# Routed expert tiles: weights split by two engines instead of three, one chunk in eight as float32

## The chip, the cores and the metric

The kernel runs on one core of a Trainium2 chip. The core has a matrix engine (TensorE, PE in the profile), three engines for elementwise work (VectorE or DVE, ScalarE or ACT, GpSimd or POOL) and SyncE (SP), whose queue issues DMAs. The metric is the time on the device in microseconds; lower is better.

## The reference

Three stages in float32: softmax attention with rotary embedding, a dense layer with softplus, and a layer in which each token whose skip score is positive goes to one of eight experts. Only the last is touched by the change:

```python
e_idx = np.argmax(xc @ w_gate, axis=1)
for e in range(E):                       # E = 8, D = 512, F = 1024
    mask = e_idx == e
    h = np.maximum(xc[mask] @ w1[e], 0.0)
    y[mask] = gate_w[mask, None] * (h @ w2[e])
out[do_compute] = xc + y
```

## The kernel before

TensorE multiplies in float32r, which keeps fewer bits than float32. So each operand is split in a high part (its float32r rounding) and a low part (the difference), and each product is three matmuls: high by high, low by high, high by low.

Attention and the dense layer take about the first 470 us. Then the tokens are sorted into tiles of 128, each of one expert (`Moe2.tiles`); nine tiles are computed. Tile 0 is begun early (`moe2.early`, lines 1156 to 1165 and 1191), tiles 1 to 8 follow in the loop of lines 960 to 979. For each tile:

- `next_w` and `load_w` load the expert's weights in eight chunks of 128 x 1024 numbers, 512 KB each, into the buffers `raw[0]` to `raw[7]`, one per chunk: 0 to 3 for the first product (L811), 4 to 7 for the second (L815). All go through SP's queue in this order: chunks 0 to 3 of the next tile, then chunks 4 to 7 of this one. A load is skipped when the expert is that of the tile before. A load waits until the buffer's last reader is done.
- `fetch` gathers the tokens' rows by an indirect DMA of GpSimd (L844), up to three tiles ahead; `gather` transposes them on TensorE (L855) and splits them (L859: high on ScalarE, low on VectorE).
- `split_w` splits each chunk into a tile `ws`. For tiles 1 to 8 the high part is a cast on ScalarE (L832), but for chunks 2, 4 and 6 on VectorE (L830). The low part is a subtraction (L836) on GpSimd for chunks 1, 3 and 5 and on VectorE for the others. The split tiles live in rings of buffers: six for chunks 0 to 3, six for 4 to 7.
- `hidden_mm` is the first product (L864): 24 matmuls of 512 columns, three for each of four chunks and two halves. `relu` (L882, ScalarE) and `turn` (transposes L893, split L895 and L896) follow.
- `result` is the second product (L910), 24 matmuls of 512 columns. `finish` makes the row numbers (L919) and the output rows (L921) on VectorE, and GpSimd scatters them by an indirect DMA (L922).

Each engine's order is not that of the text. The program is built with `schedule_with_timeline_sim=True`: a planner puts the instructions of each engine in an order by a simulated timeline, and what is under `issue_after(x)` comes after `x`. On the chip every engine then runs its list in order. In the loop, `hidden` of tile T is written before `result` of tile T - 1, and the planner mixes the two on TensorE.

Of the kernel before, what the change touches and what calls it, by code (L numbers as in the profile page):

```python
# [9 lines left out]
F32 = mybir.dt.float32  # L10
# [10 lines left out]
B, H, S, D = 2, 8, 576, 64  # L21
# [14 lines left out]
# the order in which the tiles of tokens are routed  # L36
ORDER2 = (4, 5, 6, 7, 8, 0, 1, 2, 3)
HI_DVE = (2, 4, 6)
LO_POOL = (1, 3, 5)
# [9 lines left out]
class Attention:  # L49
    """Softmax attention of head pairs; leaves x^T, split in two float32r parts, in xh and xl."""  # L50

    def __init__(self, nc, q, k, v, cst, xh, xl, pools):
        self.nc, self.q, self.k, self.v, self.cst, self.xh, self.xl = nc, q, k, v, cst, xh, xl
        self.nat, self.wq, self.wp, self.wk, self.ps_s, self.ps_t, self.ps_pv = pools
        self.pr = {}
        self.rem, self.rot = {}, {}
        self.un = {}
        self.pt = {}
        self.pv, self.sums = {}, {}
        self.qm = []  # L60
        for i in range(2):
            t = self.wq.tile([128, 2, 128], F32R, name=f"qm{i}", tag=f"qm{i}", bufs=1)
            nc.vector.memset(t.bitcast(F32), 0.0)
            nc.vector.tensor_copy(t, t.bitcast(F32))
            self.qm.append(t)
        # order of the units (query tiles of 128; "m" holds the last 64 queries of both heads)
        self.order = {0: [0, 1, 2, 3, "m"], 1: [2, 3, "m", 0, 1]}
        self.chunks = {0: [[0, 1], [2, 3, "m"]], 1: [[2, 3], ["m", 0, 1]]}
# [18 lines left out]
    # ---- loads  # L87
# [28 lines left out]
    # ---- rotary embedding  # L116
    def _rope(self, engs, out, x, tmp, cos, sin):
        """out = x * cos + swap(x) * sin, the last dimension being that of a head; the tables broadcast over heads."""
# [26 lines left out]
    # ---- transposed q, k in two parts  # L145
    def halves(self, hi, lo, src, q=False):
        """The two parts of src, which for q is scaled by 1 / sqrt(D)."""
# [30 lines left out]
    def stacks(self, b, hp):  # L178
        """Both heads' operands with K = 128: [high q; low q] against [high k; high k]."""
# [19 lines left out]
    # ---- one unit: scores, softmax  # L199
    def s_mm(self, b, hp, u, a):  # L200
# [15 lines left out]
        if (b, hp) == (0, 0) and u < 2:  # L216
            # before the stacks are there
# [41 lines left out]
    def where(self, b, u):  # L259
        """The chunk of a unit, the chunk's whole units, and where the unit's queries start in it."""  # L260
# [8 lines left out]
    def norm(self, b, hp, c):  # L269
        """1 / (sum + 1e-9) of a chunk, transposed from the rows of squares."""  # L270
# [23 lines left out]
    # ---- transposes of the probabilities, in parts, as emitters  # L294
    def t_steps(self, b, hp, u):
# [46 lines left out]
        def mk(g):  # L342
            def pe():
# [14 lines left out]
                else:  # L358
# [3 lines left out]
                    if str(g) in POOL_T[self.stage(4 * b + hp)][z]:  # L362
                        # the general purpose engine doesn't read the transposes where they are
# [15 lines left out]
    def place(self, c, i):  # L379
        """Where the chunk's two-part transposes keep block i."""  # L380
        return i if c else i - 3 * sum(3 * g < i for g in WHOLE)

    # ---- P V of one head and one chunk of queries
# [36 lines left out]
    # ---- the whole, software pipelined  # L420
    def warm(self, n, part):
        """Keeps the tensor engine's clock up while the first inputs arrive and are made ready."""
# [72 lines left out]
    def prepare(self, i, pairs):  # L495
        """What the next pair of heads needs, spread over the units of this one."""
# [24 lines left out]
class Moe1:  # L521
    """x @ w_in, softplus, @ w_out; the float64 weights are read as pairs of 32 bit words."""
# [7 lines left out]
    def weights(self, f, wp, st, bufs):  # L530
        """Loads the weights of 128 hidden units and leaves them in two float32r parts."""
# [3 lines left out]
        for i in range(2):  # L535
# [11 lines left out]
            # the float32 that keeps the first 24 bits: sign and first exponent bit, last 7 exponent bits, mantissa  # L547
# [8 lines left out]
    def hidden(self, ci, f, hp, tp, gq):  # L556
# [19 lines left out]
        # narrow chunks leave room for the logarithm beside its argument  # L576
# [9 lines left out]
        # log1p(y) = ln(u) + (y - (u - 1)) for u = y + 1 as rounded  # L586
# [29 lines left out]
class Moe2:  # L616
    """Top-1 routing of the tokens with a positive skip score; tiles of 128 tokens of one expert each."""
# [30 lines left out]
    def logits(self, t, xt, ps_a, tag="ra"):  # L648
        """Gate logits and skip score of one tile of tokens."""
# [8 lines left out]
    def route(self, t0, n, ps_a, more=None):  # L658
        """Expert, gate and rank within the expert for the tiles t0 .. t0 + n."""
# [11 lines left out]
        # the first expert among those with the largest logit, none for the tokens that skip  # L671
# [10 lines left out]
        # number of the row, zero for the tokens that skip  # L682
        nc.gpsimd.tensor_single_scalar(act, sk, 0.0, op=ALU.is_gt)
        nc.gpsimd.tensor_mul(self.tok[:, ts_, 0], c["row1"][:, ts_], act[:, :, 0])
        # ranks: earlier tokens of the tile, then of the earlier tiles
# [21 lines left out]
        # start of every tile less the full tiles of earlier tokens; token number at its place in a tile  # L707
# [14 lines left out]
        # the gate and the token's number go to the end of its row  # L722
# [13 lines left out]
    def first_tile(self, ps_a):  # L736
        """The first tile of the first expert takes tokens of the tiles routed so far; what it lacks stays empty."""
# [18 lines left out]
    def starts(self, ps):  # L756
        """Where the tokens of every expert start, and where the last ones end."""
# [12 lines left out]
    def slots(self, cum, ps_a, more):  # L770
        """The tokens of every tile and the experts of the tiles."""
        nc, c, ST, sb = self.nc, self.cst, self.ST, self.sp
        # the tile of every token: that which starts where the expert does, and the full tiles of earlier tokens on
# [6 lines left out]
        # token numbers of every tile and place; empty slots read some row and write none  # L780
# [9 lines left out]
        # experts of the tiles and their number  # L790
# [26 lines left out]
    def load_w(self, e, part, **kw):  # L817
        """Half of the weights of expert e; with a condition they may stay what they are."""
# [3 lines left out]
    def split_w(self, T, c, raw=None):  # L822
        nc = self.nc
        raw = self.raw[c] if raw is None else raw
        wp, n = self.ring[2 if c > 3 and (T, c) != (0, 4) else 0 if (c if T == 0 else 4 * T - 4 + c) % 6 < 2 else 1]
        w = wp.tile([128, 2, 2, 512], F32R, name=f"ws{T}{c}", tag="w", bufs=n).rearrange("p x a n -> p x (a n)")
        late = (T, c) in ((0, 5), (0, 6), (0, 7))
        with self.tc.issue_after(self.ex.ins) if late else nullcontext():
            if T and c in HI_DVE:
                hi = nc.vector.tensor_copy(w[:, 0], raw)  # L830
            else:
                hi = nc.scalar.copy(w[:, 0], raw)  # L832
        with self.tc.issue_after(self.late[1]) if (T, c) in ((0, 6), (0, 7)) else nullcontext():
            pool = c in LO_POOL and (T, c) != (self.NT - 1, 6) if T else c in LO0
            eng = nc.gpsimd if pool else nc.vector
# [3 lines left out]
    def fetch(self, T, xp):  # L839
        """The rows of the tokens of tile T."""  # L840
# [9 lines left out]
    def gather(self, T, xp, ps_x, tag="x"):  # L850
# [8 lines left out]
        self.split = nc.scalar.copy(xt[0], ps).ins, nc.vector.tensor_sub(xt[1], ps, xt[0].bitcast(F32)).ins  # L859
# [7 lines left out]
    def hidden_mm(self, T, st, ph):  # L867
        nc, xt = self.nc, st[1]
        for k in range(4):
            w = self.early[k] if T == 0 else self.split_w(T, k)  # L870
            for z, (x, y) in enumerate(((0, 0), (1, 0), (0, 1))):
# [55 lines left out]
    def next_w(self, T):  # L927
        """The expert of tile T, and whether it is another one than that of the tile before."""
# [5 lines left out]
    def tiles(self, Ts, xp, ps_x, ps_y, ps_h, st=None):  # L934
        """The tiles Ts; st is what hidden() left of the first one, if it has been there."""
# [24 lines left out]
        for T in Ts:  # L960
            cur = nxt
            st = self.hidden(T, st, xp, [ps_h.tile([128, 512], F32, name=f"mh{T}{c}", tag="mh") for c in range(2)])
            with ExitStack() as order:
                if first:
                    # the weights of the next tile come before what isn't needed until later
                    for done in self.did[1, 1][0], self.did[1, 1][1], self.did[1, 0][1]:
# [16 lines left out]
def constants():  # L983
# [22 lines left out]
    # number of the token on partition p of tile t, and that of its row on the way (counted from 1)  # L1006
# [30 lines left out]
def out_rows(ap, t):  # L1037
    """The rows of the tokens on partitions 0 .. 127 of tile t."""
# [7 lines left out]
def attention_moe_moe_kernel(ctx: ExitStack, tc, q, k, v, w_in, w_out, w_skip, w_gate, w1, w2, tab, out):  # L1046
# [16 lines left out]
    with ExitStack() as s1:  # L1063
# [29 lines left out]
        with ExitStack() as s2:  # L1093
# [5 lines left out]
            # the first tokens take the hidden units in two halves, the others all of them in between  # L1099
# [22 lines left out]
            def second(group):  # L1122
                """@ w_out for some steps of one phase, token tile by token tile when there are several."""
# [111 lines left out]
```

## Time and profile before

| | us |
|---|---|
| median of 3 runs | 632.38 |
| lowest, highest | 628.38, 632.98 |
| span of the profiled execution | 637.8 |
| end of the last engine's work in it | 632.8 |

The profile is of one execution. Its span is 5.4 us above the runs' median, and its last 5 us hold no work of an engine, only the branches for tiles that are not needed. Times in the views count from the span's start. In a timeline row several instructions of one kind are merged: start, time from the first to the end of the last, and their count.

### The profile page before, as it was taken

Reading aid. Unit: us, or ns where it says so; the run is one execution under the profiler, and the core shown is the slowest. Engines: PE = TensorE matmul, PEld = TensorE weight load, DVE = VectorE, ACT = ScalarE, POOL = GpSimd, SP = SyncE. Lnnn points to the kernel's source line nnn. Section 1 sums busy time; section 2 is a strip of 40 time slices with the busy share of each in tenths; the row PEclk is TensorE's granted clock in tenths of the full one; section 3 lists DMA queues with packets and bytes.
Section 4 is the critical chain, followed back from the end, with each engine's and each line's share of the span. In section 5 each row is a group of like instructions: output and inputs, shape, how many; then the busy total and the mean of one; then the engine's idle time right before and its main releaser. Section 6 shows DMA issues by size and latency. Waiting matters only on the chain. (4 is left out here: it accounts for less than half of the span.)

```text
span 637.8 us, 9087 instructions
## 1 busy us (share of the span) xinstructions
PE 562.5 (88%) x2906; PEld 444.7 (70%) x2906; DVE 520.2 (82%) x857; ACT 346.2 (54%) x795; POOL 349.7 (55%) x317
## 2 busy tenths in 40 slices
PE   5898989999999989788987799999997697997785
PEld 2576767777777766667875698898875575666663
DVE  7389887988888999998699674536867879999894
ACT  1376657777777554455455565565544273543430
POOL 5778695878443656563445742212616366574452
PEclk9699769999999989797999799999999799988788
DMA  7666260432130232433033400040246123873000
GB/s 169 160 173 162 93 167 23 121 79 63 39 71 1 67 99 69 129 122 109 2 99 103 128 34 2 6 160 6 82 168 218 49 66 125 319 249 136 2 19 30
DMA packets 40457, 62.49 MB, mean 98 GB/s; under 512 B 9313, under 2 KB 23905, under 8 KB 40401
## 3 DMA queue, kind: packets, MB, share of 16 engines
q1 hardware_dynamic: 36624, 54.88, 29.0%
q0 software_dynamic: 1440, 4.20, 1.8%
q10 hardware_dynamic: 2336, 2.74, 1.4%
q8 instruction: 26, 0.43, 0.3%
q14 instruction: 31, 0.25, 0.1%
HBM read 67.30 MB, written 7.15 MB: 117 GB/s over the span
## 5 line engine op out<-in xcount | busy, mean ns | idle before, releaser
L566 PE MATMUL h<-xh,w 128*128 128x320 f32 (+2 forms) x448 | 109.9, 327 | 5.1 <-POOL w L553 2.3
L596 POOL TENSOR_TENSOR r<-r,y 128x320 f32<-128x320 f32 (+2 forms) x54 | 56.3, 1045 | 94.4 <-DVE y L593 68.3
L610 PE MATMUL acc<-w,gh 128*128 128x512 f32 x288 | 90.3, 420 | 11.8 <-ACT gh L600 9.2
L836 POOL TENSOR_TENSOR ws<-raw,ws 128x1024 fp32r<-128x1024 f32 x25 | 65.1, 2617 | 43.3 <-ACT ws L832 22.3
L566 PEld LDWEIGHTS h<-xh,w 128*128 128x128 f32 x448 | 79.7, 198 | 12.0 <-POOL w L553 3.1
L836 DVE TENSOR_TENSOR ws<-raw,ws 128x1024 fp32r<-128x1024 f32 x42 | 76.0, 1831 | 1.0 <-ACT ws L832 0.3
L910 PE MATMUL y<-ws,hT 128*128 128x512 f32 x216 | 62.7, 431 | 14.9 <-DVE ws L836 8.9
L610 PEld LDWEIGHTS acc<-w,gh 128*128 128x128 f32 x288 | 55.0, 199 | 26.3 <-ACT gh L600 13.2
L566 PE MATMUL h<-xl,w 128*128 128x320 f32 (+2 forms) x224 | 70.1, 324 | 0.0
L553 POOL TENSOR_TENSOR w<-wt,w 128x512 fp32r<-128x512 f32 x32 | 50.1, 1568 | 32.1 <-ACT w L552 29.2
L910 PEld LDWEIGHTS y<-ws,hT 128*128 128x128 f32 x216 | 41.8, 204 | 29.2 <-DVE ws L836 12.7
L400 PE MATMUL pv<-pt,vv 128*128 128x320 f32 (+3 forms) x272 | 59.1, 338 | 2.8 <-DVE x L412 2.4
L864 PE MATMUL mh<-ws,xgT 128*128 128x512 f32 x192 | 52.5, 417 | 8.6 <-DVE ws L836 6.5
L610 PE MATMUL acc<-w,gl 128*128 128x512 f32 x144 | 51.5, 404 | 9.1 <-DVE gl L601 9.1
L239 DVE TENSOR_REDUCE m<-s 128x1 f32<-128x576 f32 x64 | 48.0, 751 | 13.1 <-PE s L231 9.5
L598 DVE TENSOR_TENSOR r<-r,u 128x320 f32<-128x320 f32 (+2 forms) x56 | 40.5, 730 | 20.3 <-POOL r L596 19.6
L252 ACT ACTIVATE P<-s,m 128x576 f32<-128x576 f32 x64 | 48.0, 750 | 9.6 <-DVE m L239 9.0
L400 PEld LDWEIGHTS pv<-pt,vv 128*128 128x128 f32 (+1 forms) x272 | 42.6, 198 | 11.6 <-issue 4.7
L864 PEld LDWEIGHTS mh<-ws,xgT 128*128 128x128 f32 x192 | 36.5, 197 | 19.5 <-DVE ws L836 9.0
L322 PE MATMUL t<-ct,P 128*128 128x128 f32 x288 | 48.6, 298 | 1.2 <-DVE pt L317 0.7
L600 ACT CAST gh<-r 128x320 fp32r<-128x320 f32 (+2 forms) x56 | 25.9, 467 | 43.7 <-DVE r L598 43.7
L832 ACT CAST ws<-raw 128x1024 fp32r<-128x1024 f32 x43 | 43.9, 1054 | 4.2 <-DMA raw<-in_moe_w_dram 2.1
(266 smaller groups left out, 1240.1 us busy)
## 6 DMA issues: line engine op xcount, KB each, us to landing
raw<-in_moe_w_dram SPq DMA_DIRECT2D x68, 512.0 KB
raw<-in_moe_w_in_dram SPq DMA_DIRECT2D x16, 512.0 KB
raw<-in_moe_w_out_dram SPq DMA_DIRECT2D x16, 512.0 KB
ks<-kT SPq DMA_DIRECT2D x32, 144.0 KB
qs<-qT SPq DMA_DIRECT2D x32, 128.0 KB
wr<-in_moe_w_dram SPq DMA_DIRECT2D x5, 512.0 KB
x2d<-x SPq DMA_DIRECT2D x9, 256.0 KB
xn<-in_q_dram SPq DMA_DIRECT2D x8, 256.0 KB
```

Source lines behind the costliest of these rows:

```text
L239: nc.vector.tensor_reduce(st["m"][:, a : a + 1], st["ps"][a][:, :, 0:288], axis=AX.XY, op=ALU.max, negate=True)
L252: nc.scalar.activation(P[:, 576 * a : 576 * a + 576].rearrange("p (c n) -> p c n", c=2), ps[:, :, 0:288], AF.Exp, bias=m[:, a : a + 1], ac ...
L322: nc.tensor.transpose(ps[:, 128 * i : 128 * i + 128], src, ident)
L400: nc.tensor.matmul(ps[:, 0:n], lhsT=vv[r, i, :], rhs=pt[r, x, self.place(c, i), 0:n], **se)
L553: nc.gpsimd.tensor_sub(w[:, i, 1, :], t, h.bitcast(F32))
L566: nc.tensor.matmul(ps[c][:, 0:m], lhsT=w[:, 0, x, 128 * k : 128 * k + 128], rhs=src[:, k, c0 + m * c : c0 + m * c + m], start=z == 0, stop ...
L596: (nc.vector if ci == 3 and f in R_DVE else nc.gpsimd).tensor_sub(r[:, c], r[:, c], y[:, c])
L610: nc.tensor.matmul(acc[t], lhsT=g[x][:, 128 * j : 128 * j + 128], rhs=w[:, 1, y, :], start=f == f0 and z == 0, stop=f == f1 and z == 2,)
L832: hi = nc.scalar.copy(w[:, 0], raw)
L836: self.did[T, c] = hi.ins, eng.tensor_sub(w[:, 1], raw, w[:, 0].bitcast(F32)).ins
L864: mm()
L910: nc.tensor.matmul(py, lhsT=ht[:, x, o : o + 128], rhs=w[:, y, 512 * j : 512 * j + 512], start=c == 0 and j == 0 and z == 0, stop=c == 3 a ...
```

## The change

For tiles 1 to 8: chunk 0 (`NATIVE`) is no longer split. `gather` keeps the first 128 columns of the transposed rows as float32 (`xr`), and `hidden_mm` multiplies them with `raw[0]` as it was loaded, in two float32 matmuls instead of six float32r ones. For the seven other chunks the high part is always made by ScalarE and the low part always by VectorE. GpSimd makes low parts for tile 0's chunks only. The ring of six buffers for the first product is counted over three chunks a tile. One of three conditions on the order of tile 0's end goes away. The rest of the diff removes comments.

```diff
-HI_DVE = (2, 4, 6)
-LO_POOL = (1, 3, 5)
+NATIVE = (0,)
...
     def split_w(self, T, c, raw=None):
         nc = self.nc
         raw = self.raw[c] if raw is None else raw
-        wp, n = self.ring[2 if c > 3 and (T, c) != (0, 4) else 0 if (c if T == 0 else 4 * T - 4 + c) % 6 < 2 else 1]
+        if T and c in NATIVE:
+            return raw
+        n1 = [x for x in range(4) if x not in NATIVE]
+        at = c if T == 0 or c > 3 else len(n1) * (T - 1) + n1.index(c)
+        wp, n = self.ring[2 if c > 3 and (T, c) != (0, 4) else 0 if at % 6 < 2 else 1]
...
-            if T and c in HI_DVE:
-                hi = nc.vector.tensor_copy(w[:, 0], raw)
-            else:
-                hi = nc.scalar.copy(w[:, 0], raw)
+            hi = nc.scalar.copy(w[:, 0], raw)
...
-            pool = c in LO_POOL and (T, c) != (self.NT - 1, 6) if T else c in LO0
-            eng = nc.gpsimd if pool else nc.vector
+            eng = nc.gpsimd if T == 0 and c in LO0 else nc.vector
...
-        self.split = nc.scalar.copy(xt[0], ps).ins, nc.vector.tensor_sub(xt[1], ps, xt[0].bitcast(F32)).ins
+        o = 0
+        if T and NATIVE:
+            xr = xp.tile([128, 128], F32, name=f"xgT{T}r", tag="gr", bufs=2)
+            nc.scalar.copy(xr, ps[:, 0:128])
+            xt.append(xr)
+            o = 128
+        self.split = (
+            nc.scalar.copy(xt[0][:, o:], ps[:, o:]).ins,
+            nc.vector.tensor_sub(xt[1][:, o:], ps[:, o:], xt[0][:, o:].bitcast(F32)).ins,
+        )
...
             w = self.early[k] if T == 0 else self.split_w(T, k)
+            if T and k in NATIVE:
+                for c in range(2):
+                    yield partial(
+                        nc.tensor.matmul, ph[c], lhsT=xt[2], rhs=w[:, 512 * c : 512 * c + 512],
+                        start=k == 0, stop=k == 3,
+                    )
+                continue
...
-                    for done in self.did[1, 1][0], self.did[1, 1][1], self.did[1, 0][1]:
+                    for done in self.did[1, 1]:
```

## Rows read from the trace of the kernel before

**Rows 1.** The page's part 1: each engine's busy us, share, instructions.

```profile
PE 562.5 (88%) x2906; PEld 444.7 (70%) x2906; DVE 520.2 (82%) x857; ACT 346.2 (54%) x795; POOL 349.7 (55%) x317
```

**Rows 2.** Windows: stretch, busy us by engine, TensorE clock, DMA share, GB/s.

```profile
596.00:614.00 18.00, 15.16 (x56) 11.88 (x56) 15.99 (x13) 6.55 (x10) 8.61 (x5) 0.81 0.04 16
...
sum 139.00, PE 114.66 PEld 87.18 DVE 127.21 ACT 57.31 POOL 75.90; mean PE 14.33 PEld 10.90 DVE 15.90 ACT 7.16 POOL 9.49
```

**Rows 3.** Groups by line and shape, 493 to 632 us: count | busy us, mean ns | idle before.

```profile
L836 DVE TENSOR_TENSOR ws<-raw,ws 128x1024 fp32r<-128x1024 f32 x39 | 72.5, 1878 | 1.0 <-ACT ws L832 0.3
...
L832 ACT CAST ws<-raw 128x1024 fp32r<-128x1024 f32 x38 | 38.9, 1055 | 2.1 <-DMA raw<-in_moe_w_dram 2.1
...
L830 DVE CAST ws<-raw 128x1024 fp32r<-128x1024 f32 x24 | 29.9, 1244 | 0.0
...
L919 DVE TENSOR_TENSOR si<-xg,e 128x1 int32<-128x1 f32 x7 | 7.9, 1131 | 1.9 <-DMA xg<-x2d,gi 1.9
...
L859 DVE TENSOR_TENSOR xgT<-xgt,xgT 128x512 fp32r<-128x512 f32 x8 | 5.4, 680 | 0.0
```

**Rows 4.** Single durations in ns, min/median/max, of tile `ws`.

```profile
L864 PE MATMUL mh<-ws,xgT x192: 387/394/793, 493.5 to 613.7; 128*128 128x512 f32 x192
...
L836 DVE TENSOR_TENSOR ws<-raw,ws x42: 1208/1226/6194, 486.5 to 627.7; 128x1024 fp32r<-128x1024 f32 x42
...
L830 DVE CAST ws<-raw x24: 675/682/3405, 495.7 to 625.9; 128x1024 fp32r<-128x1024 f32 x24
```

**Rows 5.** Timeline, 591 to 598 us: start, us, engine, line, count [idle before].

```profile
591.27 5.39 POOL L836 TENSOR_TENSOR ws<-raw,ws 128x1024 fp32r<-128x1024 f32 x2
...
592.16 2.28 DVE L830 CAST ws<-raw 128x1024 fp32r<-128x1024 f32 x1
594.47 3.27 DVE L836 TENSOR_TENSOR ws<-raw,ws 128x1024 fp32r<-128x1024 f32 x1
...
597.80 2.92 PE L910 MATMUL y<-ws,hT 128*128 128x512 f32 x6 [2.10 <-DVE ws L836]
```

**Rows 6.** Groups by line, 493 to 632 us, TensorE's two products and their idle time.

```profile
L910 PE MATMUL y<-ws,hT 128*128 128x512 f32 x195 | 57.0, 434 | 14.5 <-DVE ws L836 8.9 <-DVE ws L830 3.3 <-POOL ws L836 2.0
L864 PE MATMUL mh<-ws,xgT 128*128 128x512 f32 x192 | 52.5, 417 | 8.6 <-DVE ws L836 6.5 <-DVE xgT L859 1.1 <-POOL ws L836 1.0
```

**Rows 7.** Timeline: relu pairs of tiles 2 and 8, the last scatter.

```profile
514.00 1.10 ACT L882 ACTIVATE hs<-mh 128x512 f32<-128x512 f32 x2
...
613.92 1.08 ACT L882 ACTIVATE hs<-mh 128x512 f32<-128x512 f32 x2 [7.08 <-PE mh L864]
...
631.80 0.98 POOL L922 DMA_INDIRECT out_dram<-yo,si  x1 [4.41 <-DVE yo L921]
```

**Rows 8.** Timeline, 486 to 489 us: a gather of GpSimd beside VectorE's low parts.

```profile
486.46 3.49 DVE L836 TENSOR_TENSOR ws<-raw,ws 128x1024 fp32r<-128x1024 f32 x3
...
486.50 2.05 POOL L844 DMA_INDIRECT xg<-x2d,gi  x1 [0.30 <-issue]
```

**Rows 9.** Timeline and line 397: matmuls of float32r, of float32, and transposes.

```profile
606.64 5.25 PE L864 MATMUL mh<-ws,xgT 128*128 128x512 f32 x22
...
35.11 1.51 PE L397 MATMUL pv<-pw,vr 128*64 128x256 f32 x6
...
L397 PE MATMUL pv<-pw,vr x48: 379/379/609, 35.1 to 206.1; 128*64 128x256 f32 x48
...
546.43 1.03 PE L893 MATMUL ht<-ct,hs 128*128 128x128 f32 x8
```

**Rows 10.** DMA, 470 to 638 us in 40 slices of 4.2 us; SP's longest waits there.

```profile
GB/s 174 84 125 72 311 400 102 0 4 0 0 10 241 173 205 0 33 375 351 294 272 300 245 346 54 0 153 346 2 5 0 2 0 66 0 2 6 62 34 16
...
SPq L811 <- DVE ws L836: 24.9, 10, 5.4
```

**Rows 11.** Timeline, 491 to 512 us: the start of tile 1.

```profile
491.96 2.59 DVE L919 TENSOR_TENSOR si<-xg,e 128x1 int32<-128x1 f32 x1 [1.87 <-DMA xg<-x2d,gi]
...
496.94 7.33 DVE L836 TENSOR_TENSOR ws<-raw,ws 128x1024 fp32r<-128x1024 f32 x2
```

## The prediction

> **What bounds the kernel now.** I read the page's busy shares first [rows 1]: TensorE 88%, VectorE 82%, GpSimd 55%, ScalarE 54%. A matmul's record overlaps the next one, so these shares don't name the bound, and the diff touches only tiles 1 to 8 of the routed layer. The windows view therefore comes next, over 493 to 632 us, where those tiles run [rows 2]. There VectorE is busy 127.2 of 139 us, TensorE 114.7, ScalarE 57.3. In 596 to 614 TensorE was granted 0.81 of its clock on average, and almost no weights arrive (16 GB/s).
>
> The groups by line in that stretch [rows 3] show that VectorE's 127.2 us are not work. The undisturbed price stands in the medians [rows 4]: a low part (L836) 1.226 us, a high part (L830) 0.682 us. Line 836 has 39 low parts, so 39 x 1.226 = 47.8 us, but it took 72.5: 24.7 us too many. Line 830 has 24 high parts, 16.4 us, but took 29.9: 13.5 too many. Line 919's seven indices have one column each and took 7.9 us; I count that as waiting too. Together 46 us of 127 are waiting inside instructions. The timeline says for what [rows 5]: GpSimd runs two low parts from 591.27 to 596.66. VectorE's cast that starts at 592.16 takes 2.28 us, and its low part at 594.47 takes 3.27 and ends 1.1 us after GpSimd's last. So VectorE is held for as long as GpSimd's low part runs. TensorE then has nothing to multiply until 597.80; 2.10 us of that wait are put down to the low part, and the six matmuls after it take 2.92 us, where six take 1.55 at the spacing of [rows 9]: after the wait the clock is at its lower level, 1.2 GHz. In total [rows 6] TensorE's matmuls of these tiles have 14.5 + 8.6 = 23.1 us of idle time in front of them, and 8.9 + 3.3 + 2.0 + 6.5 + 1.0 = 21.7 of it ends with a low or high part of the weights.
>
> **The change, part by part.** Marks for the sum are the relu pairs of tile 2 (514.00) and tile 8 (613.92), and GpSimd's last scatter, ending at 632.78 [rows 7]. Between the marks lie six tile steps, 99.9 / 6 = 16.65 us each.
>
> *GpSimd's low parts go to VectorE, VectorE's high parts to ScalarE.* VectorE's stretch becomes 127.2 - 29.9 (no high parts) - 24.7 (held low parts) - 7.9 (held indices) + 20.8 (56 low parts where 39 lay in the stretch, 17 x 1.226) - 1.2 (the low part of the rows, 0.68 us, shrinks to three quarters, seven times) = 84.3 us, about 10.5 a tile. That all of the excess goes is the assumption; the other end is that only line 830's goes with its instructions and the low parts stay held by something else: 84.3 + 32.6 = 117 us, 14.6 a tile. What GpSimd keeps is indirect DMAs, and beside one of 2.05 us three low parts took 3.49 us together, undisturbed [rows 8]; I take 10.5. ScalarE gets 16 more high parts of 1.055 us [rows 3] and eight copies of 128 columns, each below such a high part of 1024: at most 57.3 + 16.9 + 8.4 = 82.6 us, 10.3 a tile. It doesn't set the pace either. Its queue is in order, though: a high part that waits for its chunk holds up the relu behind it.
>
> *One chunk in eight as float32.* Six split matmuls go, two float32 ones come. 22 matmuls of 512 columns take 5.25 us from the first to the end of the last, whose record is 0.394 us [rows 4], so one follows the other every (5.25 - 0.394) / 21 = 0.231 us [rows 9], at the upper clock level. The nearest float32 price is line 397, 256 columns: 24 matmuls leave 48 records, six in a row take 1.51 us, (1.51 - 0.38) / 5 = 0.226 us a record, 0.45 a matmul. At 512 columns that is between 0.45 (if columns cost nothing) and 0.90 (in proportion); in proportion is nearer, since all else of TensorE's goes by columns. Two cost 1.81 us where six cost 1.39: 0.42 a tile more, with ends of -0.5 and +0.42. TensorE's floor per tile is then 42 x 0.231 + 1.81 + 12 transposes x 0.13 (eight in 1.03 [rows 9]) = 9.70 + 1.81 + 1.55 = 13.0 us.
>
> The Trainium skill, page "TensorE: Matmul & The Clock Gate", section "Back-to-back issue gap", gives a sustained spacing of about 131 ns for matmuls of 512 columns in a stream with their weight loads. By that the 42 split matmuls would take an estimated 5.5 us instead of 9.7, VectorE's 10.5 us a tile would set the pace, and six steps would be 6 x (14.2 - 10.5) = 22 us shorter than in the sum below; the rows here show 231 ns, and the measurement decides.
>
> *The wait that is added.* The float32 chunk is multiplied straight from the buffer that the load fills. So on TensorE tile T's first matmul waits for a landing where it waited for a split, with all else of TensorE behind it. And on SP the load of the next tile's chunk 0 waits for TensorE's matmuls of this tile, where it waited for VectorE's low part [rows 10]; behind it on SP stand chunks 1 to 3 of the next tile and chunks 4 to 7 of this one. The time to land is covered: the load is free 1.8 us into a tile of 13.0, and eight chunks of 0.524 MB, 4.19 MB, at the 245 to 375 GB/s of the seven full slices in a row (mean 312) take 13.4 us, ends 11 and 17 [rows 10]. That about equals TensorE's 13.0 us, so in three of the six steps (transfers lie in the slices from 520 to 588 us alone) I add 1.5 us; without that cover each would cost up to the whole 13.4.
>
> *The rings.* Three split chunks a tile in the six buffers for the first product instead of four reach two tiles ahead rather than one and a half; I count nothing for it, since VectorE and not a free buffer was late. The order of the first tile's end loses one condition (the low part of chunk 0, which is no longer made): nothing, as the remaining two come later.
>
> **The sum.** *Start:* two low parts at the head of tile 1 take VectorE 7.33 us where two undisturbed ones take 2.45, and an index before it took 2.59 us [rows 11]. Without the holds 4.9 + 2.6 = 7.5 us go, but loads still land until the slice that ends at 499 [rows 10]; I take 6 us at mark tile 2 (ends 2 and 9). *Six steps:* TensorE's 13.0, plus waits that remain, between 0 and today's 23.1 / 8 = 2.9 us a tile, of which I take 0.5, because 1.4 of the 23.1 us don't end with a part of the weights and ScalarE's queue is fuller, plus 0.75 for the loads (1.5 in half the steps): 14.2 us against 16.65, a gain of 14.7 (ends: 13.0, a gain of 22; 15.9, a gain of 4.5). *End:* from mark tile 8 to the last scatter 18.9 us; 48 matmuls are 11.1, relu 1.1 [rows 7], eight transposes 1.0 [rows 9], the scatter 1.0 [rows 7], the splits and output rows, three pieces like line 859's 0.68 us [rows 3], 2.0, together 16.2; I take a gain of 2.5 us (ends 0 and 3). Sum 6 + 14.7 + 2.5 = 23.2 us. It is made against the profiled execution, whose last work ends at 632.8 us and whose span is 637.8 [rows 7]; the runs' median is 632.4. I take the gain over unchanged: **609 us**.
>
> **The rivals.**
> - *TensorE sets the pace and never waits.* For it: once fed it runs 22 matmuls without a gap. Against: [rows 2] shows 15.2 us of overlapping records in a window of 18. 632.4 - 22 - 9 - 3 = 598 us.
> - *Chunk 0's load is late in the three tiles with new weights.* SP's queue puts both halves behind TensorE; for it, SP already waits 24.9 us for splits [rows 10]; against, the load takes 13.4 us and has a tile of 14.2. At 4 us for each of three tiles: 621 us.
> - *Load and product alternate, and it ends slower.* The place is the same: if a new tile's products start only when all its chunks have landed, and the planner puts TensorE's first matmul of the tile before behind the rest of that tile's work, three tiles pay the whole 13.4 us: 609 + 40 = 649 us. It decides from 8 us a tile on (three times 8 eat the gain). Against it: the second half of the weights is not needed until the next tile's first product is through.
> - *VectorE stays held* (117 us in the stretch, above): 14.6 a tile against 16.65, no head gain but that of the index: about 619 us.
> - *Gathers starve.* An indirect DMA of GpSimd took 2.05 us beside VectorE's low parts, the last scatter, with VectorE idle, 0.98 [rows 7, 8], and VectorE now runs more of them. Gathers are issued two tiles ahead, some 28 us, so a delay by a whole run of seven low parts, 8.6 us, stays hidden unless three add up; then one shows, 618 us. The Trainium skill, "SBUF — State Buffer", section "SBUF: two separate sides", has it that GpSimd can't write the descriptors of such a DMA while VectorE runs an operation that takes the port pair which both share.
> - *No change*: the order that the planner now writes makes TensorE wait 3 us a tile more than forecast (eight tiles, 24 us): 632 us.
>
> **How the numbers follow.** The forecast (602 to 615) has 0.57, TensorE without waits 0.15 (a faster TensorE than its rows is in it, at next to nothing), the two late-load and held cases and the gathers, 616 to 626, together 0.15, no change 0.06, slower 0.07. Beyond 1% a measurement of this kernel can tell a difference (6.3 us). Faster by more: 0.57 + 0.15 + 0.15 = 0.87; within 1%: 0.06; slower: 0.07. The range runs from the floor to the far end of the late load, 598 to 623 us, and leaves out about 0.17.
>
> **What would show it.** Right: no GpSimd low part after tile 0, every VectorE low part near 1.23 us, VectorE below 92 us in the stretch, TensorE's clock above 0.95 there, relu pairs 13 to 15 us apart, float32 records of 0.43 us. Wrong: low parts that still take 2 us or more; relu pairs 17 us or more apart with TensorE waiting for chunk 0's landing; ScalarE behind every wait because its high parts stand in front of the relus; or a changed order before 485 us, where I expect none.

## The result, and the profile after

| | before | after |
|---|---|---|
| median (lowest, highest) of 4 runs, us | 632.68 (628.38, 635.64) | 598.54 (590.43, 608.9) |
| ratio of the times, 95% interval | | 0.943 (0.926 to 0.960) |
| span of the profiled execution, us | 637.8 | 588.6 |

The medians differ by 34 us; the forecast was 23. The ratio is taken from the faster executions of each kernel alone, and it makes the gain 36 us: 597 us, a little below 598, the lower end of the forecast's range. In a second measurement (among the experiments) the ratio is 0.957 (0.950 to 0.964).

Lines have moved by the diff: the high part is now L833 and the low part still L836, the gather L844, the split of the rows L866 and L867, the first product L873, the relu L898, the split of `hT` L911 and L912, the second product L926, the index L935, the scatter L938.

The page's part 1 of the changed kernel, to be held against [rows 1] (busy us, share, instructions):

```profile
PE 537.7 (91%) x2890; PEld 424.4 (72%) x2890; DVE 476.6 (81%) x849; ACT 361.5 (61%) x819; POOL 289.5 (49%) x293
```

Whole-kernel shares again say little: VectorE has the same share as before. The windows of the routed tiles say more. Windows of the changed kernel, tiles 1 to 8 (stretch, length, busy us of PE, PEld, DVE, ACT, POOL, then TensorE's granted clock, DMA share, GB/s), which answer to [rows 2]:

```profile
478.00:513.00 35.00, 33.80 (x150) 25.11 (x149) 29.81 (x37) 27.25 (x37) 4.25 (x4) 1.00 0.33 114
513.00:548.00 35.00, 35.00 (x164) 27.30 (x163) 26.63 (x30) 23.57 (x34) 8.11 (x5) 1.00 0.87 310
548.00:583.00 35.00, 33.26 (x146) 25.26 (x144) 27.96 (x31) 22.48 (x30) 5.73 (x4) 1.00 0.11 40
sum 105.00, PE 102.06 PEld 77.68 DVE 84.40 ACT 73.30 POOL 18.08; mean PE 34.02 PEld 25.89 DVE 28.13 ACT 24.43 POOL 6.03
```

The work that took 139 us takes 105. VectorE is busy 84.4 us instead of 127.2, although it makes 56 low parts there instead of 39. TensorE is busy throughout the middle window, and its granted clock is 1.00 in all three, the upper level of 2.4 GHz, where [rows 2] had 0.81 in a stretch with waits.

Groups by line and shape in the same stretch (count | busy us, mean ns | idle before), which answer to [rows 3] and [rows 6]:

```profile
L836 DVE TENSOR_TENSOR ws<-raw,ws 128x1024 fp32r<-128x1024 f32 x56 | 66.5, 1221 | 8.7 <-ACT ws L833 8.6
L833 ACT CAST ws<-raw 128x1024 fp32r<-128x1024 f32 x55 | 55.4, 1057 | 6.1 <-DMA raw<-in_moe_w_dram 6.0
L926 PE MATMUL y<-ws,hT 128*128 128x512 f32 x193 | 51.4, 407 | 0.1
L873 PE MATMUL mh<-ws,xgT 128*128 128x512 f32 x144 | 37.5, 407 | 0.0
...
L855 PE MATMUL xgt<-ct,xg 128*128 128x128 f32 x24 | 3.6, 275 | 1.2 <-DVE hT L912 1.2
...
L935 DVE TENSOR_TENSOR si<-xg,e 128x1 int32<-128x1 f32 x9 | 1.3, 154 | 4.5 <-DMA out_dram<-yo,si 4.5
```

A low part takes 1.221 us on average where it took 1.878, an index 0.154 us where it took 1.131. Ahead of TensorE's two products stand 0.1 us of idle time where 23.1 stood. Now VectorE is the one that waits: 8.6 us for ScalarE's high parts. That delays hardly anybody: TensorE waits for VectorE once, for 1.2 us, ahead of the transposes of tile 3's rows (L855).

Timeline of the changed kernel: a float32 chunk, the relu pairs of tiles 2 and 8, the last scatter (start, us, engine, line, count, idle before), beside [rows 7]:

```profile
482.04 1.88 PE L873 MATMUL mh<-raw,xgT2r 128*128 128x512 f32 x4
...
490.83 1.11 ACT L898 ACTIVATE hs<-mh 128x512 f32<-128x512 f32 x2
...
568.72 1.09 ACT L898 ACTIVATE hs<-mh 128x512 f32<-128x512 f32 x2 [2.57 <-PE mh L873]
...
582.43 0.98 POOL L938 DMA_INDIRECT out_dram<-yo,si  x1 [4.26 <-DVEq L1217]
```

The six steps between the relu pairs take 568.72 - 490.83 = 77.9 us, 12.98 each, where they took 99.9. From the mark of tile 8 to the end of the last scatter it is 14.7 us where it was 18.9. The third piece is the start: from the first cast of tile 0's `hT` (470.27 after, 484.64 before) to the mark of tile 2, 20.6 us where it was 29.4. The routed stage as a whole, first cast to last scatter, went from 148.1 to 113.1 us: **35.0 us, of which the start has 8.8, the six steps 22.0, the end 4.2**.

What the 22.0 us of the six steps are made of, two windows between the marks show, the first of the kernel before, the second of the kernel after:

```profile
514.00:614.00 100.00, 85.35 (x362) 64.71 (x360) 96.11 (x77) 44.90 (x62) 59.80 (x28) 0.93 0.42 146
490.80:568.70 77.90, 76.70 (x348) 58.99 (x348) 64.32 (x73) 56.05 (x78) 14.77 (x9) 1.00 0.52 186
```

TensorE's idle time falls from 14.7 to 1.2 us, which is 13.5 of the 22. The other 8.6 us are time in which it was busy: 85.35 us before and 76.70 after, although the float32 chunk adds some 2 us. That goes with the granted clock, 0.93 before and 1.00 after. So a wait can cost twice: after the one of [rows 5] that ends at 597.80, the granted clock is at its lower level (0.50, 1.2 GHz) until 603.

The first cast itself comes 14.4 us earlier, though the change touches nothing ahead of it. It goes with the granted clock of an execution, not with the change (first pair of experiments).

### The profile page after: what moved, and what is told of

The parts are those of the page before. It is cut to its first block, busy times and chain, and to the rows that moved or that the text cites. A ratio compares the mean times of both kernels' runs of the same rounds, so it can differ in the third digit from the quotient of the medians.

```text
span 588.6 us, 9059 instructions
## 1 busy us (share of the span) xinstructions
PE 537.7 (91%) x2890; PEld 424.4 (72%) x2890; DVE 476.6 (81%) x849; ACT 361.5 (61%) x819; POOL 289.5 (49%) x293
## 5 line engine op out<-in xcount | busy, mean ns | idle before, releaser
L566 PE MATMUL h<-xh,w 128*128 128x320 f32 (+2 forms) x448 | 106.7, 320 | 5.1 <-POOL w L553 2.3
L566 PEld LDWEIGHTS h<-xh,w 128*128 128x128 f32 x448 | 76.8, 191 | 12.0 <-POOL w L553 3.1
L836 DVE TENSOR_TENSOR ws<-raw,ws 128x1024 fp32r<-128x1024 f32 x58 | 68.9, 1221 | 8.7 <-ACT ws L833 8.6
L833 ACT CAST ws<-raw 128x1024 fp32r<-128x1024 f32 x59 | 59.4, 1057 | 6.4 <-DMA raw<-in_moe_w_dram 6.0
L926 PE MATMUL y<-ws,hT 128*128 128x512 f32 x216 | 57.8, 409 | 0.1
L938 POOL DMA_INDIRECT out_dram<-yo,si x9 | 14.1, 1567 | 88.3 <-DVE yo L937 80.5
L594 ACT ACTIVATE u<-u 128x320 f32<-128x320 f32 (+2 forms) x56 | 26.5, 480 | 36.0 <-DVE y L593 28.3
L322 PE MATMUL t<-ct,P 128*128 128x128 f32 x288 | 45.7, 283 | 2.7 <-DVE kT L154 1.5
L926 PEld LDWEIGHTS y<-ws,hT 128*128 128x128 f32 x216 | 39.6, 189 | 10.9 <-issue 1.7
L566 PEld LDWEIGHTS h<-xl,w 128*128 128x128 f32 x224 | 42.2, 191 | 2.5
```

The costliest lines, as they stand in the source:

```text
L322: nc.tensor.transpose(ps[:, 128 * i : 128 * i + 128], src, ident)
L566: nc.tensor.matmul(ps[c][:, 0:m], lhsT=w[:, 0, x, 128 * k : 128 * k + 128], rhs=src[:, k, c0 + m * c : c0 + m * c + m], start=z == 0, stop ...
L836: self.did[T, c] = hi.ins, eng.tensor_sub(w[:, 1], raw, w[:, 0].bitcast(F32)).ins
L926: nc.tensor.matmul(py, lhsT=ht[:, x, o : o + 128], rhs=w[:, y, 512 * j : 512 * j + 512], start=c == 0 and j == 0 and z == 0, stop=c == 3 a ...
```

## The experiments

The theory: a GpSimd low part holds VectorE's instruction until it is done; with GpSimd out of the splits VectorE's work fits beside TensorE's, and TensorE then sets the pace. Rivals: the float32 chunk brings the gain by saving splits (A); what was gained is lost GpSimd work and not a lost hold (B); the loads still show in the tile steps (C); the profile after was a lucky execution (D).

The same marks in every kernel (us; low parts are VectorE's L836, median and longest, ns):

| kernel | first cast at | start | six steps | end | routed stage | low parts |
|---|---|---|---|---|---|---|
| before | 484.6 | 29.4 | 99.9 | 18.9 | 148.1 | 1226, 6194 |
| before, again | 477.0 | 30.0 | 100.6 | 18.9 | 149.5 | longest 6179 |
| after | 470.3 | 20.6 | 77.9 | 14.7 | 113.1 | 1220, 1228 |
| after, again | 474.3 | 21.7 | 77.5 | 14.7 | 114.0 | longest 1227 |
| after, no float32 chunk | 474.0 | 22.4 | 75.6 | 14.7 | 112.7 | 1218, 1227 |
| before, float32 chunk alone | 481.9 | 28.4 | 92.9 | 18.5 | 139.8 | longest 8735 |
| after, three float32 chunks | 471.2 | 21.9 | 80.9 | 13.9 | 116.8 | 1221, 1227 |
| after, float32 in tiles 1, 2 | 479.8 | 21.6 | 75.9 | 14.7 | 112.2 | longest 1226 |
| after, no new weights | 470.3 | 21.8 | 77.5 | 14.7 | 114.0 | 1220, 1227 |
| after, GpSimd subtracts | 481.9 | 30.8 | 88.4 | 14.7 | 133.8 | 1420, 2462 |
| after, GpSimd fills | 484.0 | 30.2 | 78.9 | 14.7 | 123.8 | 1219, 1564 |
| after, GpSimd scales | 475.9 | 33.4 | 97.5 | 14.7 | 145.6 | 1232, 1655 |
| after, GpSimd subtracts late | 482.9 | 21.5 | 82.2 | 14.8 | 118.6 | 1218, 2914 |

### Both kernels once more

The kernel before, unchanged:

> The kernel before, unchanged, for a second profile. In the profile of before the last work ends at 632.8 us, and tile 0's first cast of the second product (L895) starts at 484.6; in that of after it starts at 470.3, although the instructions up to there stand in the same order. If that 14 us is the clock of one execution (granted 0.87 in before's first 130 us, 0.97 in after's first 350), this profile will put it anywhere between 468 and 486, with the mean clock moving along, and the stretch from there to the last scatter stays near 148 us. If it belongs to the kernel before (something that the change moves early on), it stands at 483 to 486 again. Time 626 to 637 us either way.

636.0 us (median of 4), the kernel before measured beside it 633.6. The first cast comes at 477.0 instead of 484.6 us with the same program, at a mean granted clock of 0.949 for the execution instead of 0.928. The kernel after, unchanged:

> The changed kernel once more, unchanged. If the routed stage is paced by TensorE at its floor, its marks come out again: start 20.6 us, six steps 77.9 us, end 14.7 us, each within 0.7 us, wherever the stage begins. If the first profile was a lucky execution, the six steps take 80 us or more. The total is expected at 597 us, ratio 0.943.

598.6 us beside 629.2, ratio 0.957 (0.950 to 0.964). Five of its six steps come out to 0.02 us as in the first profile; the other, from tile 2 to tile 3, is 0.4 us shorter, and the start is 1.2 us longer, more than the 0.7 that I had allowed. Rival D falls. So the routed stage repeats to 1.4 us or better in either kernel, while the first cast lies anywhere between 470 and 485 us in the kernels of the table. It goes with TensorE's granted clock ahead of it: in the seven profiles in which that was 0.95 or more (0.957 in the kernel before, again; 0.972 in the kernel after) the first cast comes at 470.3 to 477.0 us, in the six with 0.94 or less (0.933 in the kernel before) at 479.8 to 484.6. What sets the clock of an execution no run shows. The routed stage gives 35 us, the two ratios 36 and 27 us; what the ratios differ by I have not traced. In the experiments below the routed stage is therefore the measure, and not the total.

### The float32 chunk

The kernel after, with every chunk split:

```diff
-NATIVE = (0,)
+NATIVE = ()
```

> After, but with chunk 0 split like the others: the engines are reassigned, nothing is multiplied as float32. Theory (GpSimd's low parts held VectorE, and with them gone TensorE alone sets the pace): TensorE's floor falls from 13.0 to 48 x 0.231 + 1.55 = 12.6 us a tile, VectorE's work rises to 11.7 and ScalarE's to 11.1, so the time stays within 6 us of after's, 592 to 604 us, and relu pairs stay near 13 us apart. Rival (the float32 chunk carries the gain by relieving both splitting engines): most of the gain goes, 615 us or more, relu pairs 15 us apart or more.

597.4 us, ratio 0.946 (0.938 to 0.954): the same as with the float32 chunk. The six steps are 1.9 to 2.3 us shorter than in the two profiles of the kernel after, 0.33 to 0.39 a tile; the start is 0.7 to 1.9 us longer. The other half is chunk 0 in float32 with the other seven chunks divided over three engines as in the kernel before:

```diff
...
-            hi = nc.scalar.copy(w[:, 0], raw)
+            hi = nc.vector.tensor_copy(w[:, 0], raw) if T and c in HI_DVE else nc.scalar.copy(w[:, 0], raw)
...
-            eng = nc.gpsimd if T == 0 and c in LO0 else nc.vector
+            eng = nc.gpsimd if (c in LO_POOL if T else c in LO0) else nc.vector
```

> After, but the seven split chunks keep before's engines: high parts of chunks 2, 4, 6 on VectorE, low parts of 1, 3, 5 on GpSimd. Theory: VectorE loses one low part of 1.23 us a tile and is held as before by three GpSimd low parts, so of 16.65 us a tile at most 1.2 to 2 us go: 615 to 625 us, with VectorE low parts of 3.3 us in the trace. Rival (the float32 chunk carries the gain): 596 to 605 us.

628.9 us (616.5 to 630.3) beside 633.6, where I had expected 615 to 625; the routed stage takes 139.8 us instead of 148 to 150. So alone the float32 chunk is worth some 9 us there; once the hold is gone it is worth nothing. VectorE is busy 8.9 us less in the stage than in the kernel before (124.2 us, 133.1 before), and 6.4 of that are its high parts, which are held for less (23.5 us, 29.9 before). Its low parts, fewer and longer (34 of 2.21 us in the mean, not the 3.3 expected, where 42 took 1.83), take as much as before. Rival A falls. Three chunks in float32:

```diff
-NATIVE = (0,)
+NATIVE = (0, 1, 2)
...
-            xr = xp.tile([128, 128], F32, name=f"xgT{T}r", tag="gr", bufs=2)
-            nc.scalar.copy(xr, ps[:, 0:128])
+            xr = xp.tile([128, 384], F32, name=f"xgT{T}r", tag="gr", bufs=2)
+            nc.scalar.copy(xr, ps[:, 0:384])
...
```

> After with chunks 0, 1 and 2 as float32 instead of chunk 0 alone; VectorE and ScalarE lose two parts a tile each. Theory: each more such chunk costs TensorE 0.42 us a tile and nothing else counts, so the six steps between the relu pairs of tiles 2 and 8 go from 77.9 to 77.9 + 6 x 2 x 0.42 = 82.9 us; time 600 to 608. Rival (VectorE or ScalarE is still part of the pace): the steps stay below 78.

601.6 us, ratio 0.968 (0.957 to 0.979). The six steps grow by 3.0 us (3.4 against the second profile of the kernel after) and not by 5, which is 0.25 to 0.28 us for each further chunk and tile. TensorE's 1.2 us of idle time between the marks is gone here, so that its matmuls alone cost 0.35 a chunk. Windows of this kernel:

```profile
490.00:520.00 30.00, 30.00 (x128) 20.61 (x127) 20.59 (x26) 18.73 (x29) 5.64 (x4) 1.00 0.40 119
520.00:550.00 30.00, 30.00 (x123) 20.78 (x122) 18.52 (x23) 17.49 (x25) 4.51 (x3) 1.00 0.87 304
```

VectorE is down to 18.5 of 30 us and TensorE is as busy as ever, and the steps get longer: work taken off VectorE buys no more than that 1.2 us, and the added matmuls cost more. Chunk 0 in float32 only where VectorE was thought to be late, in tiles 1 and 2 (with the ring of the first product counted over four chunks from tile 3 on):

```diff
...
-        if T and c in NATIVE:
+        if 0 < T <= LAST and c in NATIVE:
...
```

> The changed kernel, with chunk 0 as float32 in tiles 1 and 2 only; in tiles 3 to 8 all eight chunks are split. If the float32 chunk pays only where VectorE is late, that is at the start, the start (first cast of tile 0's products to the relu pair of tile 2) is 20.6 us as in the changed kernel, and the six steps after it take 75.6 us as without any float32 chunk: the routed stage takes about 111 us where the changed kernel took 113.1, 2.3 us less, 0.4% of the total. If VectorE's eighth low part a tile makes TensorE wait, the six steps take 78 us or more and nothing is gained.

596.6 us, ratio 0.945 (0.938 to 0.952), beside 0.957 (0.950 to 0.964) for the kernel after, measured at the same time. The routed stage is 112.2 us, 1 to 2 below the kernel after, 0.5 below no float32 chunk at all; as times these can't be told apart. The start was 21.6, not 20.6.

### What holds VectorE

The kernel after, in which GpSimd subtracts to no purpose in each of tiles 1 to 8:

```diff
+    for z in range(IDLE if T else 0):        # IDLE = 6, called at the end of gather
+        x = self.ring[2][0].tile([128, 512], F32, name=f"idle{T}{z}", tag="idle", bufs=1)
+        self.nc.gpsimd.tensor_sub(x, xg[:, 0:512], xg[:, 0:512])
```

> After, plus six subtractions of 128 x 512 a tile on GpSimd (about 1.4 us each, 8.2 us a tile, near the 7.8 of before's three low parts), on the gathered rows into a tile that nobody reads. The orders of TensorE, VectorE and ScalarE stay those of after; the output is the reference's. Theory (a GpSimd subtraction holds VectorE's two-input operations for as long as it runs, whoever needs its result): VectorE's 10.5 us a tile and the 8.2 add up, its low parts again show 2 to 4 us, the relu pairs go to 15 to 18 us apart and the time to 615 to 645 us. Rival (before, the low parts that GpSimd made were late for TensorE themselves, and the hold cost nothing): nobody waits for these, so after's time within 6 us, 592 to 604.

622.4 us, ratio 0.989 (0.977 to 1.001). Of the routed stage's 35 us, 20 are gone (133.8 us), with no work taken from or given to VectorE, ScalarE or TensorE; some more of the total lies ahead of the first cast, which comes at 481.9 us in this profile. Durations of tile `idle` and of VectorE's low parts (ns, min/median/max):

```profile
L1226 POOL TENSOR_TENSOR idle<-xg x48: 1038/1901/1970, 488.4 to 578.5; 128x512 f32<-128x512 f32 x48
...
L836 DVE TENSOR_TENSOR ws<-raw,ws x58: 1206/1420/2462, 483.8 to 610.7; 128x1024 fp32r<-128x1024 f32 x58
```

The low parts stretch to 1.56 us on average, and the subtractions on GpSimd from 1.04 (the shortest) to 1.90 (the median): both sides wait. But the start is 9 to 10 us longer as well, and that has a second cause. This kernel's waits, 480 to 620 us (us in total, times, longest):

```profile
DVE si L935 <- DMA out_dram<-yo,si: 13.9, 2, 8.4
```

Gathers and scatters stand in GpSimd's queue behind the added work, and VectorE's next index waits for them. Two more kernels, each run once, vary the kind of work. Sixteen fills of 128x512 and one scaling a tile:

```diff
...
+        self.nc.gpsimd.memset(x, 0.0) if z else self.nc.gpsimd.tensor_scalar(x, xg[:, 0:512], 1.0, 1.0, op0=ALU.mult, op1=ALU.mult)
```

> After, plus GpSimd work that reads nothing from SBUF: a tile 17 operations, one copy and 16 fills of 128 x 512, into a tile that nobody reads. If any GpSimd operation holds VectorE: its low parts again show 1.6 us or more in the mean and the stretch from tile 0's L911 to the last scatter goes from 113 toward the 134 us of the run with idle subtractions. If only GpSimd operations that read SBUF hold it, as the Trainium skill has it ("SBUF — State Buffer", section "SBUF: two separate sides"): low parts of 1.22 us, the stretch within 3 us of 113.

615.4 us in one run. Twelve scalings a tile, with one input each:

```diff
...
+        self.nc.gpsimd.tensor_scalar(x, xg[:, 0:512], 1.0, 1.0, op0=ALU.mult, op1=ALU.mult)
```

> After, plus GpSimd work with one SBUF input: 12 scalings of 128 x 512 a tile, some 0.7 us each, 8 us a tile, into a tile that nobody reads. If an operation with one input holds VectorE as one with two does: low parts of 1.5 us or more in the mean, the stretch from tile 0's L911 to the last scatter 125 to 136 us. If only two-input GpSimd operations hold it: low parts of 1.22 us, the stretch within 3 us of 113.

629.0 us in one run. Durations in these two kernels, the fills' first:

```profile
L1226 POOL MEMSET idle<- x128: 524/526/552, 491.2 to 587.2; 128x512 f32 x128
...
L836 DVE TENSOR_TENSOR ws<-raw,ws x58: 1214/1219/1564, 485.8 to 602.7; 128x1024 fp32r<-128x1024 f32 x58
```

```profile
L1226 POOL TENSOR_SCALAR idle<-xg x96: 617/636/1669, 482.4 to 598.3; 128x512 f32<-128x512 f32 x96
...
L836 DVE TENSOR_TENSOR ws<-raw,ws x58: 1206/1232/1655, 477.7 to 616.4; 128x1024 fp32r<-128x1024 f32 x58
```

128 fills leave the low parts at 1.219 us, and the one of 1.564 overlaps a scaling; 96 scalings bring them to 1.41 on average. So VectorE's subtractions are held by GpSimd instructions that read, and not by GpSimd's being busy. VectorE's casts of weights, which were held too in the kernel before [rows 5], don't run in these kernels. The Trainium skill, "SBUF — State Buffer", section "SBUF: two separate sides", says that an operation of VectorE with two inputs in SBUF contends only with a GpSimd operation that reads SBUF, and that the later of the two waits for the whole of the other; the durations of these kernels agree. The stage is longer with the fills nevertheless, which is the second cause again: the six steps take 78.9 us, 1.0 to 1.4 more than in the kernel after, but the start takes 30.2, and VectorE waits 20.0 us in three waits for indices behind late indirect DMAs. With the scalings it waits 37.3 us in six, so hold and late DMAs can't be told apart in that kernel's time. I had not foreseen this when I put the idle work into `gather`. The last of the four takes it away: four subtractions of 128x1024 in tiles 6 and 7 only, from the relu's output, when the last gather has been issued; VectorE's order differs in one exchange of neighbours, TensorE's and ScalarE's in nothing.

```diff
+    for z in range(IDLE if T in (6, 7) else 0):      # IDLE = 4, called at the head of turn
+        x = self.ring[2][0].tile([128, 1024], F32, name=f"idle{T}{z}", tag="idle", bufs=1)
+        self.nc.gpsimd.tensor_sub(x, st[1], st[1])
```

> The changed kernel, with four GpSimd subtractions of 128x1024 each in tiles 6 and 7, from the relu's output into a tile that nobody reads. The last gather of rows stands ahead of all of them on GpSimd, the orders on TensorE, ScalarE and SyncE are those of the changed kernel, and VectorE's differs in one exchange of neighbours. If a GpSimd subtraction holds VectorE's, the VectorE low parts beside it take 2.5 to 3.3 us instead of 1.22 and TensorE waits for them: the steps between the relu pairs 6 to 7 and 7 to 8 are 15 to 17 us each instead of 13.0, while the steps 2 to 6 stay at 13.0; in total 4 to 8 us more than the changed kernel. If the earlier runs with idle GpSimd work were slow only because gathers stood behind it, the low parts stay at 1.22 us, all six steps at 13.0, and the total within 1 us of the changed kernel.

608.1 us (597.4 to 609.3), beside 598.6 (595.1 to 603.7) for the kernel after; these times overlap and don't decide, and this profile's first cast comes at 482.9 us. Its routed stage is 4.6 us longer than in the second profile of the kernel after, at a granted clock of 1.00 in both. The steps are 13.6, 12.7, 13.7, 12.8, then 13.4 and 16.0, where the kernel after, again, has 13.6, 12.7, 13.7, 12.8, then 12.8 and 11.9. Timeline of this kernel in its last step:

```profile
570.38 8.02 DVE L836 TENSOR_TENSOR ws<-raw,ws 128x1024 fp32r<-128x1024 f32 x4
571.64 3.06 PE L926 MATMUL y<-ws,hT 128*128 128x512 f32 x12 [0.86 <-DVE ws L836]
571.81 11.17 POOL L1226 TENSOR_TENSOR idle<-hs 128x1024 f32<-128x1024 f32 x4 [0.94 <-ACT hs L898]
...
578.92 2.31 DVE L836 TENSOR_TENSOR ws<-raw,ws 128x1024 fp32r<-128x1024 f32 x1
...
581.28 1.66 PE L873 MATMUL mh<-ws,xgT 128*128 128x512 f32 x6 [0.43 <-DVE ws L836]
581.76 2.31 DVE L836 TENSOR_TENSOR ws<-raw,ws 128x1024 fp32r<-128x1024 f32 x1
...
584.12 1.65 PE L873 MATMUL mh<-ws,xgT 128*128 128x512 f32 x6 [1.17 <-DVE ws L836]
```

This is the picture of [rows 5] again: low parts of 2.3 to 2.9 us under the subtractions, and TensorE waiting for them. My expectation missed the first of the two steps, which grew by 0.6 us only and not by 2 or more: three low parts there took 2.0 to 2.2 us, but TensorE waited just 0.3 us for them. That the hold makes TensorE wait is shown, and rival B falls: nothing was taken off GpSimd here but put on it. How much of the 35 us is the hold's alone isn't shown. The change also moves VectorE's high parts to ScalarE, and no run moves only these or only GpSimd's low parts.

### The loads

The kernel after, in which no tile counts as of a new expert, so that tiles 1 to 8 multiply by weights that are there already:

```diff
-        nc.vector.tensor_tensor(et[:, 25:41], et[:, 1:17], et[:, 0:16], op=ALU.not_equal)
+        nc.vector.tensor_tensor(et[:, 25:41], et[:, 1:17], et[:, 1:17], op=ALU.not_equal)
```

> After, but no tile from 1 on loads new weights (all of them use those of expert 0, so tiles of other experts are computed with the wrong weights); every order stays that of after. Theory (TensorE alone sets the pace, the loads lie wholly beside it): relu pair of tile 2 to that of tile 8 takes 77.9 us as in after, within 1 us; time 590 to 603. Rival (the loads still cost what the prediction put down for them, 1.5 us in three tiles, hidden in after's 77.9): 73.4 us or less between those marks, and the time some 4 us lower.

597.7 us, ratio 0.963 (0.950 to 0.975). One window of this kernel, and the same of the kernel after:

```profile
520.00:550.00 30.00, 30.00 (x140) 23.16 (x139) 22.46 (x26) 20.46 (x30) 4.93 (x3) 1.00 0.06 20
```

```profile
520.00:550.00 30.00, 30.00 (x139) 22.86 (x138) 24.22 (x27) 21.44 (x30) 4.93 (x3) 1.00 0.90 320
```

With 20 GB/s instead of 320 TensorE is as busy as before, and the six steps are 77.5 us against 77.5 to 77.9. The start and the end don't change either. Rival C falls: these loads are hidden.

## Why the prediction was right and wrong

**Right: what bounded the kernel.** VectorE was held inside its instructions, and TensorE starved behind it. In the changed kernel the low parts take 1.22 us as their median of [rows 4] said, an index 0.15, VectorE is busy 84.4 us in the stretch, where the sum said 84.3 and the bound 92, and TensorE's clock is 1.00. That 84.3 and 84.4 come so near each other is luck: the sum left out the indices' own 1.3 us, and the low parts in the window take 66.5 us where it had 68.6.

**Right: the float32 chunk.** Four records in 1.88 us, (1.88 - 0.59) / 3 = 0.43 us each, as forecast. The measured price is 0.33 to 0.39 us a tile against a chunk split (0.42 forecast), 0.25 to 0.35 for each of two more.

**Right: TensorE's floor.** 13.0 us forecast; the steps measured 12.98, of which 0.2 is the wait ahead of tile 3's rows, so that the floor itself was 0.2 lower than forecast. The rule of the Trainium skill by which a matmul would follow every 131 ns (page "TensorE: Matmul & The Clock Gate", section "Back-to-back issue gap") does not show: at 42 x 0.131 the steps could not have stood at 12.98 us with TensorE busy for all but 1.2 of 77.9 us.

**Wrong: what comes on top of the floor.** The sum took 14.2 us a tile, the floor plus 0.5 for waits that remain and 0.75 for loads. The waits that remain measured 0.2 us a tile (the one of 1.2 us), the loads nothing: the steps don't change when the loads go. With the floor's 0.2 that is 6 x (14.2 - 12.98) = 7.3 us of the 11.8 by which the stage's gain of 35.0 exceeds the forecast's 23.2; the start has 2.8 of them, the end 1.7. For the waits I had leant on the 1.4 of 23.1 us of before that don't end with a part of the weights, and on ScalarE's fuller queue. But VectorE is busy 10.7 and ScalarE 9.3 us in 13, and buffers for more than a tile lie between them and TensorE; with that room only 0.2 of the 2.9 us a tile were left. The waiting does go on, on VectorE, which waits 8.6 us for high parts, where TensorE doesn't feel it. For the loads I had the transfer's 13.4 us beside a tile of 13.0 and counted a late landing. SP's loads of the next tile do wait for TensorE now, as I wrote (waits of SP's queue, 470 to 588 us, after; us in total, times, longest):

```profile
SPq L811 <- PE mh L873: 24.0, 5, 7.6
```

and ScalarE's high parts wait 6.0 us for landings, five times. These chunks are late for ScalarE, and through it for VectorE; no wait of TensorE stands behind them.

**Too small: the start and the end.** The start gained 8.8 us, and 7.6 with the second profile of the kernel after, where 6 were taken; 7.5 us was the forecast's own count of the holds there, from which I took off for loads. Without new weights the start is 21.8 us, as with them (20.6 and 21.7), so that deduction was for nothing. The end gained 4.2 where I took 2.5. There the sum of 16.2 us laid the relu and the splits of tile 8 end to end with the matmuls. After the mark, TensorE runs 48 matmuls and eight transposes with 0.1 us of gaps; the relu and splits lie under matmuls of tile 7.

**The rivals.** What came is the one that had 0.15: TensorE sets the pace and hardly ever waits, 598 us. Its gains of 22, 9 and 3 us measured 22.0, 8.8 and 4.2. Its steps were worked out right, and what spoke against it (15.2 us of overlapping records in 18) was the state with the hold, no evidence on the state without. The late load, the alternation of load and product and the held VectorE did not come. Gathers did not starve behind VectorE: they take 1.0 to 1.5 us where they took up to 2.05 [rows 8]. The scatters do take longer, 1.73 us in the median instead of 1.19, but no wait of TensorE names them. What makes indirect DMAs late is GpSimd's own work, which the experiments put back.

**Ahead of the stage.** I forecast no change before 485 us; the instructions stand there in the same order, and the first cast still moved by 14 us from one profile to the other. The second profile of the kernel before shows 7.6 us of that without any change.

## What to carry to other kernels

If the median of an instruction lies far below its mean (1.226 and 1.878 us here), look for the engine whose instruction ends together with the long ones: moving the work to the held engine can be cheaper than sharing it. Once the new pace-setter is named and all engines that feed it need clearly less per step, with buffers for a step between, take its floor as the forecast and today's leftover waits as the unlikely end. And test a suspected contention with idle work, but put it where no DMA of the same engine stands behind it.

## What the runs showed of the hardware

- GpSimd instructions that read hold VectorE's two-input subtraction, those with one input too (mean 1.41 us instead of 1.22); fills do not (1.226, and the one long low part lies beside a scaling). The other way a 128x512 subtraction on GpSimd goes from 1.04 to 1.90 us.
- Beside back-to-back subtractions of 128x1024 on GpSimd, a low part of 1.22 us takes up to 2.9 us: the two engines take turns.
- Beside low parts of VectorE a scatter of GpSimd took 1.71 to 1.74 us (seven of the kernel after), with VectorE idle 0.98 (its last).
- The same program reached the first cast of tile 0 at 484.6 and at 477.0 us, with TensorE's granted clock ahead of it at 0.933 and 0.957.
